# A pruned linear layer on one core: tile 7 of x loaded from GpSimd's queue, and one more late tile stored in halves

## Chip, core and metric

The kernel runs on one core of a Trainium2 chip. A core has a matrix engine (TensorE, "PE" in the profile), a vector engine (VectorE, DVE), a scalar engine (ScalarE, ACT), GpSimd (POOL) and SyncE (SP), and 16 DMA engines that move data between HBM and the on-chip memory (SBUF). Each of SP, ACT and POOL can issue transfers; all of them run on the same 16 DMA engines. The metric is device microseconds for one execution, the median of several runs.

## What is computed

The weights w (1024 x 1024, bf16) are pruned 2:4: of every four consecutive rows, each column keeps the two entries with the largest magnitude. Then x (16 x 512 tokens of 1024 features) is multiplied by the pruned weights and the bias is added.

```python
wg = w.reshape(G, M, D)                 # D = 1024, M = 4, G = 256
mag = jnp.abs(wg)
order = jnp.argsort(mag, 1)
thr = jnp.take_along_axis(mag, order[:, M - N:M - N + 1, :], 1)    # N = 2
mask = (mag >= thr)
wp = (wg * mask).reshape(D, D)
return jnp.einsum("bsd,df->bsf", x, wp) + b
```

## The kernel before

The 8192 tokens are 64 tiles of 128. PE multiplies one tile by the 1024 x 1024 weights in 16 matmuls (eight blocks of 128 features by two halves of 512 output columns), with fp32 sums in PSUM; DVE adds the bias and writes bf16 (`evac`, L400), and ScalarE issues the store of the tile.

Before that can run in a steady loop the weights must be loaded, pruned by DVE and laid out. The prologue works on six pieces of w, numbered 0 to 5: (rows 0 to 511, columns 0 to 255), (the same rows, 256 to 511), and so on. Piece 0 is loaded as four transfers of 64 KB, one for each of the four members m of a group ("u, v, s, t"), two issued by SP and two by ScalarE (L110 to L113). DVE computes magnitudes, maxima, minima, threshold, mask and product of each piece; the product of the first member is the step `mult0u`, written to `wp`.

So that PE has work while later pieces are pruned, the first eight tiles of tokens ("early tiles", 0 to 7) take piece 0 and 1 and so on as they come. Their x is loaded as it lies in HBM, only features 0 to 511 (`load_x`, L103), transposed by PE against an identity matrix into PSUM (`transpose`, L184, the steps "T"), copied to SBUF by ScalarE (`copy_xt`, L192, the steps "C"), and multiplied (`mm_piece`, L205, the steps "M"; M7.0u is tile 7 by the first member of piece 0). Only two PSUM banks serve the transposes, so a third transpose waits for the copy of the first. The x loads of the early tiles are tile 7 (ScalarE), tiles 0 and 1 (ScalarE), tiles 5 and 6 (SP), tile 4 (SP), tiles 2 and 3 (SP). Tiles 5 to 7 are interleaved in groups of three rows in HBM, so that tile 7 is 128 rows of 1 KB.

The order of the work is written out by hand for every engine (`order`, L258) and the program order of each engine is held by `seq` (L64), which also covers the DMA issues of `issue` (L96). PE's list begins

```python
"F8 T7a T5a T6a M7.0u M5.0u M7.0v M5.0v T1a M6.0u M6.0v T0a M7.0s M5.0s M6.0s M7.0t ..."
```

F8 and the calls at L370 and L371 are "fillers": matmuls on constants that give PE something to do from the start. Tile 7 is the first that PE transposes. `make_identity` (L128) makes the identity on GpSimd, with a memset and a select. GpSimd has nothing else to do until it adds the bias to parked sums at L396.

After the prologue, tiles 12 to 63 come in batches, transposed by the DMA on load (`load_nat`, L374). In the last part the loop at L437 stores each tile with one transfer of 256 KB, except that a tile t with t >= NT - LATE is stored in two halves of 512 columns, each as soon as its half is evacuated (L457). The last tile, 63, is cut into four stores. LATE is 5, so tiles 59 to 62 go in halves, and tile 63 in its four parts.

Of the kernel before, what the change touches and what calls it, by code (L numbers as in the profile page):

```python
# [10 lines left out]
def kernel(  # L11
# [7 lines left out]
    nc = tc.nc  # L19
# [20 lines left out]
    NPK = 8  # L40
    LEAD = 4
    GROUPS = ((0, 5), (5, 8))
    LATE = 5
    sizes = (4, 8, 8, 8, 8, 8, 8)
    batches = []
    t0 = NPK + LEAD
# [17 lines left out]
    def seq(eng, inst):  # L64
        if eng in tails:
            tc.add_manual_dep(inst.ins, tails[eng].ins.name, NOSYNC, reason="program order")
        tails[eng] = inst
        return inst
# [22 lines left out]
    def tokens(dram, t):  # L91
        a, b_ = next(s for s in GROUPS if s[0] <= t < s[1])
        return dram[a * P:b_ * P].rearrange("(p t) k -> p t k", p=P), t - a
    bias_sb = const.tile([P, Dout], bf16)

    def issue(eng, out_, in_):  # L96
        q = nc.sync if eng == "sp" else nc.scalar
        return seq(eng, q.dma_start(out_, in_))  # L98

    def load_w(g, c0, c1, ma=0, mb=4, eng="sp"):  # L100
        issue(eng, w_sb[:, g, ma:mb, c0:c1], wv[:, g, ma:mb, c0:c1])

    def load_x(ta, tb, eng="sp"):  # L103
        xs = const.tile([P, tb - ta, HK], bf16, name=f"x_{ta}")
        xv, n = tokens(xf, ta)
        issue(eng, xs[:], xv[:, n:n + tb - ta, :HK])
        for t in range(ta, tb):
            x_sb[t] = xs[:, t - ta, :]

    load_w(0, 0, 256, 0, 1)  # L110
    load_w(0, 0, 256, 1, 2, "act")
    load_w(0, 0, 256, 2, 3)
    load_w(0, 0, 256, 3, 4, "act")  # L113
    load_x(7, 8, "act")
    load_x(0, 2, "act")
    act(nc.scalar.activation(spark[:], nc.const_aps.tensor(1.0, [P, 1], bf16), Act.Abs))
    load_x(5, 7)
# [21 lines left out]
    def spread(g, c0, c1, ks=range(4), eng="sp"):  # L139
        for k in ks:  # L140
            issue(eng, wp_nat[:, 4 * g + k, c0:c1], wp[32 * k:32 * k + 32, g, :, c0:c1])
# [256 lines left out]
    def evac(o, ps, c0, c1, add=None):  # L398
        if add is None:
            dve(nc.vector.tensor_tensor(o[:, c0:c1], ps, bias_sb[:, c0:c1], op=Alu.add))  # L400
        else:
            dve(nc.vector.tensor_tensor(o[:, c0:c1].rearrange("p (n c) -> p n c", n=2),  # L402
                                        ps.rearrange("p (n c) -> p n c", n=2), add, op=Alu.add))
# [7 lines left out]
    def store(eng, t, o, c0=0, c1=Dout):  # L411
        issue(eng, rows(t)[:, c0:c1], o[:, c0:c1])
# [24 lines left out]
    for bi, (tb, nb) in enumerate(batches):  # L437
        if bi:
            load_batch(bi + 1)
        for j in range(nb):  # L440
# [9 lines left out]
            else:  # L450
# [4 lines left out]
                for h in range(2):  # L455
                    evac(o, pss[h][:], h * FH, (h + 1) * FH)
                    if t >= NT - LATE:  # L457
                        store("act", t, o, h * FH, (h + 1) * FH)
                if t < NT - LATE:
                    store("act", t, o)  # L460
# [30 lines left out]
```

## Time and profile before

| | |
|---|---|
| timed runs | 233.79, 233.35, 233.44 us; median 233.44 |
| the profiled execution | 233.83 us, of which the span from first to last instruction is 232.0 us |
| granted TensorE clock | 1.000 (mean) |
| instructions | 2851 |
| HBM read, written | 3.41 MB, 16.78 MB |
| issues of stores `out_dram<-o` | 59 of 256 KB and 8 of 128 KB on ScalarE, 1 of 128 KB on SP, and the small ones of tile 63 |
| x loads | 256 KB by SP twice, 128 KB by SP, 256 KB by ScalarE, 128 KB (tile 7) by ScalarE |

How to read it: the page gives for each engine its busy time and share of the span; for the engines' waits, the time in which an engine was idle and what ended the wait; a chain of waits that is followed back from the last instruction; a timeline of instructions with their start and duration in microseconds from the span's start; and, for stretches of the span, the busy time of each engine and the busy share and rate of the DMA. "L98" is line 98 of the kernel. `SPq` and `ACTq` are the issuing of transfers, `PEld` the weight loads of PE, which overlap its matmuls. The trace also records when each transfer's semaphore increments arrive, that is, when it has landed.

### The profile page before, as it was taken

How to read it: one execution, taken by the hardware profiler on the slowest of the kernel's cores; microseconds unless marked ns; L12 is line 12 of the kernel's file. 1: busy time of each engine (PE TensorE's matmuls, PEld its weight loads, DVE VectorE, ACT ScalarE, POOL GpSimd, SP SyncE). 2: the span in 40 equal slices, each digit the busy share in tenths (PEclk: the TensorE clock that was granted, in tenths of full speed). 3: DMA queues.
4: the chain of work that ended last, by engine and by line, in shares of the span. 5: the costliest groups of instructions: out<-in, count | busy, mean ns of one | idle time of the engine just before them, and what ended most of it. 6: DMA issues, size and time to landing. Idle time of an engine off the chain costs nothing.

```text
span 232.0 us, 2851 instructions
## 1 busy us (share of the span) xinstructions
PE 228.0 (98%) x1158; PEld 112.7 (49%) x1158; DVE 107.9 (46%) x188; ACT 13.4 (6%) x27; POOL 17.6 (8%) x15
## 2 busy tenths in 40 slices
PE   8999999999999999999999999999999999999995
PEld 4887444544444444444444444444444444444443
DVE  4999767754234334334334324424424424423434
ACT  2665100000000000000000000000000000000000
POOL 1000199700000000000000000000000000000000
PEclk9999999999999999999999999999999999999999
DMA  6999999997299321992249821697229942122122
GB/s 192 354 220 211 220 213 227 300 241 272 94 198 275 114 93 51 234 275 76 90 99 250 239 93 47 169 230 198 84 90 191 242 155 76 63 90 81 60 88 90
DMA packets 78268, 38.19 MB, mean 165 GB/s; under 512 B 63664, under 2 KB 70576, under 8 KB 78256
## 3 DMA queue, kind: packets, MB, share of 16 engines
q1 hardware_dynamic: 67328, 20.61, 43.7%
q10 hardware_dynamic: 10928, 17.40, 21.1%
q8 instruction: 9, 0.15, 0.3%
q14 instruction: 3, 0.02, 0.0%
HBM read 3.41 MB, written 16.78 MB: 87 GB/s over the span
## 4 chain that ended last, share of the span: by engine, by line
PE 96%; DMA 2%; ACTq 0%; ACT 0%; DVE 0%; issue 0%
PE ps L239 88%; PE ps L216 6%; DMA x<-in_x_dram 2%; PE tp L239 1%; PE tp L189 1%; ACTq L98 0%; ACT xt L194 0%; DVE o L400 0%
## 5 line engine op out<-in xcount | busy, mean ns | idle before, releaser
L239 PE MATMUL ps<-wp_nat,xb 128*128 128x512 bf16 (+2 forms) x848 | 179.8, 375 | 0.0
L239 PEld LDWEIGHTS <-xb 128*128 128x128 bf16 x848 | 82.4, 98 | 97.5
L400 DVE TENSOR_TENSOR o<-ps,bias_sb 128x512 bf16<-128x512 f32 (+1 forms) x112 | 71.5, 677 | 114.6 <-PE ps L239 114.5
L396 POOL TENSOR_TENSOR st<-st,bias_sb 128x1024 f32<-128x1024 f32 x8 | 16.8, 2131 | 0.0
L216 PE MATMUL ps<-wp,xt 128*128 128x256 bf16 x128 | 15.1, 273 | 0.0
L239 PE MATMUL ps<-wp_nat,xlow 128*128 128x512 bf16 x64 | 14.1, 379 | 0.0
L216 PEld LDWEIGHTS <-xt 128*128 128x128 bf16 x128 | 12.2, 98 | 1.8 <-ACT xt L194 0.2
L402 DVE TENSOR_TENSOR o<-ps,st 128x512 bf16<-128x512 f32 x16 | 11.1, 691 | 2.8 <-PE ps L239 2.3
L239 PE MATMUL ps<-wp_nat,xlead 128*128 128x512 bf16 x48 | 11.2, 379 | 0.0
L239 PEld LDWEIGHTS <-xlow 128*128 128x128 bf16 x64 | 7.2, 112 | 6.7
L239 PEld LDWEIGHTS <-xlead 128*128 128x128 bf16 x64 | 6.3, 98 | 7.1
L256 ACT COPY st<-ps 128x512 f32<-128x512 f32 x16 | 8.5, 598 | 6.3 <-PE ps L216 4.3
L154 DVE TENSOR_TENSOR mag<-mag,hi 128x256 bf16<-128x256 bf16 (+3 forms) x10 | 5.6, 582 | 0.2
L154 DVE TENSOR_TENSOR wp<-w_sb,mag 128x256 bf16<-128x256 bf16 (+3 forms) x10 | 5.6, 580 | 0.1
L133 PE MATMUL ps<-const-bfloat16-1.0 128*128 128x128 bf16 (+1 forms) x22 | 4.3, 394 | 0.8 <-PEq L475 0.8
L164 DVE TENSOR_SCALAR mag<-w_sb 128x512 uint16<-128x512 uint16 (+2 forms) x6 | 2.7, 464 | 3.3 <-DMA w_sb<-in_w_dram 3.3
L239 PE MATMUL tp<-wp_nat,xlead 128*128 128x512 bf16 x16 | 4.1, 379 | 0.0
L133 PEld LDWEIGHTS <-const-bfloat16-1.0 128*128 128x128 bf16 x22 | 2.5, 147 | 2.4 <-issue 2.4
L189 PE MATMUL tp<-ident,x 128*128 128x128 bf16 x32 | 2.9, 219 | 0.6 <-DMA x<-in_x_dram 0.4
L154 DVE TENSOR_TENSOR hi<-mag 128x512 bf16<-128x512 bf16 (+2 forms) x7 | 3.2, 459 | 0.1
L154 DVE TENSOR_TENSOR lo<-mag 128x512 bf16<-128x512 bf16 (+2 forms) x7 | 3.2, 456 | 0.0
L194 ACT COPY xt<-tp 128x256 f32<-128x256 f32 x8 | 2.8, 381 | 3.5 <-PE tp L189 3.5
(15 smaller groups left out, 13.4 us busy)
## 6 DMA issues: line engine op xcount, KB each, us to landing
out_dram<-o ACTq DMA_DIRECT2D x59, 256.0 KB, 2.4
wp_nat<-wp SPq DMA_DIRECT2D x14, 128.0 KB, 3.5
w_sb<-in_w_dram SPq DMA_DIRECT2D x3, 512.0 KB, 6.4
out_dram<-o ACTq DMA_DIRECT2D x8, 128.0 KB, 1.7
x<-in_x_dram SPq DMA_DIRECT2D x2, 256.0 KB, 4.0
w_sb<-in_w_dram SPq DMA_DIRECT2D x1, 256.0 KB, 5.0
x<-in_x_dram ACTq DMA_DIRECT2D x1, 256.0 KB, 4.1
bias_sb<-in_b_dram SPq DMA_DIRECT2D x1, 256.0 KB, 6.4
```

The source lines that it names most:

```text
L133: pe(nc.tensor.matmul(warm_ps[:, :rep * P], lhsT=nc.const_aps.tensor(1.0, [P, P], bf16), rhs=nc.const_aps.tensor(1.0, [P, rep * P], bf16), ...
L154: dve(nc.vector.tensor_tensor(out, a, b_, op=op))
L164: dve(nc.vector.tensor_single_scalar(self.mag[:, ms, :].bitcast(u16), self.w[:, ms, :].bitcast(u16), 0x7FFF, op=Alu.bitwise_and))
L189: pe(nc.tensor.transpose(tp[:, m, :], xg[:, m, :], ident[:]))
L194: act(nc.scalar.copy(xt[:].bitcast(fp32), xpk[t].bitcast(fp32)))
L216: pe(nc.tensor.matmul(ps[:, c0 + d:c1 + d], lhsT=xpk[t][:, m, :], rhs=wp[:, g, m, c0:c1], start=(new and m == ms.start), stop=(left[(q, n) ...
L239: pe(nc.tensor.matmul(ps, lhsT=xt[:, kt - koff, :], rhs=wp_nat[:, kt, c0:c1], start=(kt == first), stop=(kt == last)))
L256: act(nc.scalar.copy(st[:, n % 2, :, :].rearrange("p t c -> p (t c)"), ps_open.pop((q, n))[:]))
L396: pool(nc.gpsimd.tensor_tensor(st[:], st[:], bias[:, :, None, :].to_broadcast([P, 2, 2, CW]), op=Alu.add))
L400: dve(nc.vector.tensor_tensor(o[:, c0:c1], ps, bias_sb[:, c0:c1], op=Alu.add))
L402: dve(nc.vector.tensor_tensor(o[:, c0:c1].rearrange("p (n c) -> p n c", n=2), ps.rearrange("p (n c) -> p n c", n=2), add, op=Alu.add))
```

## The change

Three edits. `issue` learns a third queue, GpSimd's. The load of tile 7 is issued from that queue, and stands first among the loads instead of fifth, where it was the third transfer that ScalarE issued. And LATE goes from 5 to 6, so that tile 58 is stored in halves too.

```diff
-    LATE = 5
+    LATE = 6
...
     def issue(eng, out_, in_):
-        q = nc.sync if eng == "sp" else nc.scalar
+        q = {"sp": nc.sync, "act": nc.scalar, "pool": nc.gpsimd}[eng]
         return seq(eng, q.dma_start(out_, in_))
...
+    load_x(7, 8, "pool")
     load_w(0, 0, 256, 0, 1)
     load_w(0, 0, 256, 1, 2, "act")
     load_w(0, 0, 256, 2, 3)
     load_w(0, 0, 256, 3, 4, "act")
-    load_x(7, 8, "act")
     load_x(0, 2, "act")
     act(nc.scalar.activation(spark[:], nc.const_aps.tensor(1.0, [P, 1], bf16), Act.Abs))
     load_x(5, 7)
```

## The prediction

> **What bounds the kernel now.** First the busy rows of the page: PE is busy 228.0 of 232.0 us, so only time in which PE waits, or its start, can be won.
>
> ```profile
> PE 228.0 (98%) x1158; PEld 112.7 (49%) x1158; DVE 107.9 (46%) x188; ACT 13.4 (6%) x27; POOL 17.6 (8%) x15
> ```
>
> Then the waits of PE. From 11 to 229 us the list is empty; all that there is lies before 11 us:
>
> ```profile
> PE tp L189 <- DMA x<-in_x_dram: 0.4, 1, 0.4
> PE tp L189 <- ACT xt L194: 0.2, 1, 0.2
> ```
>
> So the end is the start of PE's real work plus a fixed stretch of matmuls. The chain of waits, cut to its first 8 us, says what sets that start (start us, us, what):
>
> ```profile
> 0.74 0.41 ACTq L98
> ...
> 1.18 0.46 ACTq L98
> ...
> 1.66 3.79 DMA x<-in_x_dram
> ...
> 5.50 0.43 PE tp L189 x4
> ...
> 5.95 0.38 ACT xt L194
> ...
> 6.38 0.38 PE tp L189 x4
> 6.76 0.44 PE ps L216 x4
> ```
>
> ScalarE issues two pieces of w and then tile 7 of x (at 1.66); that lands at 5.46, PE transposes tile 7 (T7, 5.50), tile 5 (T5), then waits for the copy C7, which frees a PSUM bank, transposes tile 6 (T6, 6.38) and starts the first real matmul, M7.0u, at 6.60. The last filler starts at 4.89 and the next instruction could follow at 4.94. So T7 can move by at most 5.50 - 4.94 = 0.56 us.
>
> Third, the timeline of DVE, because M7.0u also needs the first product mult0u:
>
> ```profile
> 3.27 0.29 DVE L164 TENSOR_SCALAR mag<-w_sb 128x512 uint16<-128x512 uint16 x1 [3.27 <-DMA w_sb<-in_w_dram]
> 3.59 0.29 DVE L154 TENSOR_TENSOR hi<-mag 128x256 bf16<-128x256 bf16 x1
> 3.80 0.29 DVE L164 TENSOR_SCALAR mag<-w_sb 128x512 uint16<-128x512 uint16 x1
> ...
> 5.99 0.48 DVE L154 TENSOR_TENSOR wp<-w_sb,mag 128x256 bf16<-128x256 bf16 x2
> ```
>
> DVE starts when w rows 0 and 1 are in (the second landed at 3.24), and never waits again before 5.99. Its first multiply runs 5.994 to 6.276. That is the second gate, hidden by 0.3 us today.
>
> Fourth, the DMA in stretches of the start (last two columns: busy share of the 16 DMA engines, GB/s):
>
> ```profile
> 2.20:2.90 0.70, 0.70 (x4) 0.19 (x2) 0.00 (x0) 0.26 (x1) 0.00 (x0) 1.00 1.16 315
> 2.90:3.30 0.40, 0.40 (x3) 0.12 (x2) 0.03 (x1) 0.40 (x1) 0.00 (x0) 1.00 0.72 170
> 3.30:3.80 0.50, 0.50 (x6) 0.50 (x5) 0.47 (x2) 0.50 (x1) 0.00 (x0) 1.00 0.89 276
> ```
>
> The engines are full while the w pieces move (2.2 to 2.9), have room from 2.9 to 3.8, and are full again later (358 GB/s from 5.5 to 7.5). An early tile 7 is not free: its 131 KB must pass somewhere.
>
> **The change, step by step.** *Removed:* the issue of tile 7 from ScalarE's queue, 0.454 us. Tiles 0 and 1, issued behind it, go from 2.15 to about 1.66; they landed at 6.26 and were used at 6.93 (slack 0.67): no gain by themselves. The two w issues ahead of it stay.
>
> *Added:* the same 128 rows of 1 KB issued by GpSimd, first thing behind the opening barrier, at about 0.73. No row of before shows a GpSimd transfer. From below: issued by SP at 0.73, a load's first packet moved at 1.82, on ScalarE (0.74) at 2.0; no row has GpSimd quicker than those, so first packets from about 1.9 on. From above: the slowest load of the prologue took 7.2 us to land, so 7.9 at worst in these rows. Nearest is the hardware issue, with some GpSimd work on top (its select over 128x128 took 0.29 us, a 128x1024 add 2.13): I take first packets at 2.4. Eight packets per DMA engine in turn with two other queues (46 + 27 + 27 ns a round) are 0.8 us, and w row 0 landed 0.35 after its last packets: landed at 3.5, give or take 0.5. Anything landed by 4.9 is as good as immediate, for PE is in its fillers until 4.94.
>
> Behind it on GpSimd are only the memset and the select of the identity (0.73 to 1.31 today); T7 needs them at 4.94, so the issue may hold GpSimd 3.6 us at no cost. The bias adds come at 28 us.
>
> *PE after that:* T7 at 4.94, and C7 copied at 5.39 to 5.77 (the copy starts 0.45 after T7 and takes 0.375). T5 needs tiles 5 and 6, landed at 5.15 today: 5.20 (its copy ends 0.85 later and is used at 6.38, so 5.5 would do). T6 at 5.82, and M7.0u would be free at 6.04. Now mult0u ends at 6.276, and with 0.05 us of signal (the copy C7 ended at 6.328, T6 started at 6.379) M7.0u starts at 6.33 instead of 6.60. **The most that the move can win is 0.27 us, not 0.56**; DVE is the bound behind the load. T7 could even start at 5.23 for that.
>
> *Does 0.27 reach the end?* The waits behind M7.0u, their slack from event times in the trace: next multiply 0.34, tile 0 0.67, third multiply 0.62, pieces 1, 2 and 3 of the weights 1.23, 0.97 and 1.18, the spread of piece 3 0.99. Two short waits on C copies (0.18 at 9.86, 0.11 at 10.63) belong to PE's own order and move along. So 0.27 would be kept.
>
> *The price on w.* If tile 7's packets fall between those of w, w lands later by up to 131 KB / 315 GB/s = 0.42 us; by its packets, 8 per DMA engine of 46 ns each, 0.37. Call the delay of DVE's start d; the gain is 0.27 - d. Packets before 2.1 give d = 0.37 to 0.42, a loss of 0.10 to 0.15. At 2.4 us ScalarE's queue had started 78 packets, of 128 for w row 1, so row 1 is late by 0.14; rows 2 and 3 come late by 0.37, but DVE starts on them at 3.80 and they landed by 3.59, so 0.18 of that is covered: d = 0.19. From about 2.8 on, tile 7 falls into the room up to 3.8: d = 0. I take 0.19: gain 0.08.
>
> The Trainium skill speaks against this change: "DMA: Bandwidth & Descriptors", section "Rules for kernel authors", says that spreading transfers over SP, ACT and GpSimd brings no bandwidth and only saves issue time. The 1.16 share at 2.2 to 2.9 agrees with it, the 0.72 right after does not. By the rule alone d would be near 0.4 and the gain gone; by the row alone it is 0.27 for a late enough start.
>
> *SP's queue.* Plain loads take eight semaphores in turn, and the ninth (tile 4) waited for the first: SP stood 0.48 us before 3.26. If tile 7 leaves the turn, tile 4 is the eighth and goes at 2.8; the bias no longer waits for tile 7 (5.46 landed, 5.47 issued). Later loads go up to 0.4 earlier, but behind the same SP loads as now, and their users have the slacks above: 0.
>
> *Tile 58 in halves:* one more issue of 0.338 us on ScalarE, whose queue has 3.45 us per tile there and computes nothing; the first half leaves 0.65 us earlier (one 512-column add). The last landing belongs to tile 63, issued at 229.75. DVE and PE do not wait on stores at the end: 0. The closing list of waits on SP gets one more entry, for GpSimd's transfer; the last such step today took 0.065 us (231.224 to 231.289): 0 to 0.07, and mostly done before the last store lands: 0.
>
> **Sum.** 0.08 us off the profiled execution: span 232.0 to 231.9, its own time 233.83 to 233.75. The three timed runs have a median of 233.44, 0.39 below that execution; the same step from there gives **233.36, say 233.35**.
>
> **Rivals.**
> *A, w is hit in full:* GpSimd is as quick as the hardware queues. For it: the full engines at 2.2 to 2.9. d = 0.37 to 0.42, 233.54 to 233.59. 12%.
> *B, w is not hit:* packets start at 2.8 or later and land by 5.2. For it: the room at 2.9 to 3.8, and that GpSimd's rows are long beside other engines' (that add of 2.13 us). 0.27 off, 233.17. 25%.
> *C, GpSimd is late, the slower side:* the move replaces T7's wait by a longer one for the same tile. It loses from a landing past 5.46 on, one for one, since everything behind it is PE's own order; past 5.93 it is more than 0.47 us (0.2%, about what a measurement of this kernel can tell from no change). With the slowest prologue load's 7.2 us: landed 7.9, +2.5, 235.9. For it: no GpSimd transfer in the trace shows that it is quick. Against: tile 7 has a queue of its own and little to move. 18%.
> The skill's "GPSIMD Engine Reference", section "Instruction dispatch", gives about 6 us for the first call of freshly loaded code; no run here shows it for a transfer, and by it alone (an estimate) tile 7 would land near 9 and the time be about 237.
> *D, the move does not do what it says:* another load lands last. Tiles 5 and 6 share the engines with tiles 0 and 1 earlier; if they come at 5.7 instead of 5.15, T5 goes to 5.75, as today, and all is back at 233.44. Against: less is ahead of them. 5%.
> My forecast has 37%, and 3% are left for a gain over 0.47, for which I see no mechanism.
>
> **Numbers.** B, the forecast, A and D lie within 0.2%: 79%; C nearly all slower. With some room for errors between sessions: faster 0.04, same 0.78, slower 0.18. The range goes from 232.95 (B and 0.2 of scatter; the three runs span 0.44) to 233.95, which takes in the first half microsecond of C.
>
> **What would show it.** After: T7 right behind the fillers near 4.95; no PE wait on x; T6 near 5.8; then PE waits for DVE's wp ahead of M7.0u, which it never did before. DVE's first instruction later than 3.27 by d; M7.0u at 6.33 + d. ScalarE's third issue at 1.66 is tiles 0 and 1; tile 4 at 2.8. PE without waits from 11 us on. Wrong would be: PE waiting for x past 5.46, a wait for the identity, M7.0u ahead of 6.3, or a new wait past 11 us.

## The result, and the profile after

| | before | after |
|---|---|---|
| median of 22 runs each, same chip and session | 233.68 us (233.26 to 234.25) | 234.56 us (233.94 to 236.47) |
| ratio, 95% interval | | 1.0048 [1.0037, 1.0060] |
| the profiled execution, its span | 233.83, 232.0 us | 234.10, 232.3 us |

The change made the kernel slower by about half a percent. The profiled execution of after is one of its quicker ones (0.46 us under the median), so the trace explains the first 0.27 us of the loss and not all of it; more on that below.

First the busy rows and the waits of PE. PE's busy time hardly differs, and there is still no PE wait behind 11 us; the wait for the copy is gone from this list, and the wait for x has doubled from 0.4 to 0.8 us (columns: total, times, longest, in us).

```profile
PE 227.9 (98%) x1158; PEld 112.5 (48%) x1158; DVE 108.0 (47%) x188; ACT 13.4 (6%) x27; POOL 18.3 (8%) x16
```

```profile
PE ps L133 <- PEq L475: 0.8, 1, 0.8
PE tp L189 <- DMA x<-in_x_dram: 0.8, 1, 0.8
```

The chain of waits of after, cut to its first 8 us (start us, us, what):

```profile
0.74 0.39 SPq L98
...
1.19 0.42 SPq L98
...
1.66 4.30 DMA x<-in_x_dram
...
6.00 0.43 PE tp L189 x4
...
6.46 0.38 ACT xt L194
...
6.88 0.50 PE ps L216 x3
```

Before, the chain began on ScalarE's queue (`ACTq`) and its transfer was tile 7. Now it begins on SP's, and the transfer issued at 1.66 is that of tiles 5 and 6. It lands at 5.96, where it landed at 5.15 before. The timeline of PE shows what that does. First before, then after:

```profile
5.50 0.64 PE L189 MATMUL tp<-ident,x 128*128 128x128 bf16 x8 [0.38 <-DMA x<-in_x_dram]
6.38 0.38 PE L189 MATMUL tp<-ident,x 128*128 128x128 bf16 x4 [0.24 <-ACT xt L194]
```

```profile
4.85 0.38 PE L189 MATMUL tp<-ident,x 128*128 128x128 bf16 x4
6.00 0.64 PE L189 MATMUL tp<-ident,x 128*128 128x128 bf16 x8 [0.77 <-DMA x<-in_x_dram]
6.48 0.91 PE L216 MATMUL ps<-wp,xt 128*128 128x256 bf16 x4
```

T7 runs at 4.85, 0.65 earlier than before. Then PE stands until 6.00 for tile 5 (before: T5 at 5.75). M7.0u is even a little earlier (6.48 against 6.60), but M5.0u needs C5, the copy of tile 5, which runs from 6.46 to 6.83. PE's wait for it stands in no list: the views show the matmuls of L216 as one stretch of 0.91 us. By the single matmuls in the trace M5.0u starts at 6.884 instead of 6.708: **0.18 us later**. From there PE's own order carries it to the end: the first matmul of L239 goes from 21.55 to 21.74, the last from 229.17 to 229.36, both 0.19 later. What follows the last matmul took 4.66 us of the profiled execution before and 4.74 after. 0.19 + 0.08 = 0.27, the difference of the two profiled executions.

Two more views. The timeline of GpSimd shows the new transfer and what stands behind it:

```profile
1.23 0.68 POOL L98 DMA_DIRECT2D x<-in_x_dram  x1 [0.78 <-POOLq L475]
1.90 0.22 POOL masks.py:197 MEMSET ident<- 128x128 bf16 x1
2.20 0.29 POOL masks.py:199 TENSOR_SCALAR_AFFINE_SELECT ident<-ident 128x128 bf16<-128x128 bf16 x1
```

And the start of DVE's timeline and its first product, with the DMA in the three stretches that the prediction read (last two columns: busy share of the 16 DMA engines, GB/s):

```profile
3.01 0.29 DVE L164 TENSOR_SCALAR mag<-w_sb 128x512 uint16<-128x512 uint16 x1 [3.01 <-DMA w_sb<-in_w_dram]
...
5.80 0.48 DVE L154 TENSOR_TENSOR wp<-w_sb,mag 128x256 bf16<-128x256 bf16 x2
```

```profile
2.20:2.90 0.70, 0.70 (x4) 0.18 (x2) 0.00 (x0) 0.70 (x1) 0.29 (x1) 1.00 0.99 250
2.90:3.30 0.40, 0.40 (x3) 0.12 (x2) 0.29 (x1) 0.40 (x1) 0.00 (x0) 1.00 1.31 268
3.30:3.80 0.50, 0.50 (x6) 0.50 (x5) 0.47 (x3) 0.35 (x2) 0.00 (x0) 1.00 0.77 215
```

w is not late: DVE starts at 3.01 (3.27 before; 3.06 in e1 below, where the loads stand as before, so this is scatter and no gain of the move). GpSimd's first packet moves only at 2.84, when w has nearly passed. Nor is tile 7 late: landed at 4.57, used at 4.85. The transfer that was moved did what it was meant to do. The one beside it became late.

### The profile page after: what moved, and what is told of

It is laid out like the page before. It is cut to its first block, busy times and chain, and to the rows that moved or that the text cites. A ratio compares the mean times of both kernels' runs of the same rounds, so it can differ in the third digit from the quotient of the medians.

```text
span 232.3 us, 2854 instructions
## 1 busy us (share of the span) xinstructions
PE 227.9 (98%) x1158; PEld 112.5 (48%) x1158; DVE 108.0 (47%) x188; ACT 13.4 (6%) x27; POOL 18.3 (8%) x16
## 3 DMA queue, kind: packets, MB, share of 16 engines
HBM read 3.41 MB, written 16.78 MB: 87 GB/s over the span
## 4 chain that ended last, share of the span: by engine, by line
PE 96%; DMA 2%; SPq 0%; ACT 0%; issue 0%; DVE 0%
PE ps L239 88%; PE ps L216 6%; DMA x<-in_x_dram 2%; PE tp L239 1%; PE tp L189 1%; SPq L98 0%; ACT xt L194 0%; DVE o L400 0%
## 5 line engine op out<-in xcount | busy, mean ns | idle before, releaser
L239 PE MATMUL ps<-wp_nat,xb 128*128 128x512 bf16 (+2 forms) x848 | 179.8, 375 | 0.0
L239 PEld LDWEIGHTS <-xb 128*128 128x128 bf16 x848 | 82.4, 98 | 97.5
L216 PE MATMUL ps<-wp,xt 128*128 128x256 bf16 x128 | 15.2, 273 | 0.1
L239 PE MATMUL ps<-wp_nat,xlow 128*128 128x512 bf16 x64 | 14.1, 379 | 0.0
L216 PEld LDWEIGHTS <-xt 128*128 128x128 bf16 x128 | 12.2, 98 | 2.1 <-ACT xt L194 0.6
L239 PE MATMUL ps<-wp_nat,xlead 128*128 128x512 bf16 x48 | 11.2, 379 | 0.0
L239 PEld LDWEIGHTS <-xlow 128*128 128x128 bf16 x64 | 7.2, 112 | 6.7
L239 PEld LDWEIGHTS <-xlead 128*128 128x128 bf16 x64 | 6.2, 98 | 7.1
L239 PE MATMUL tp<-wp_nat,xlead 128*128 128x512 bf16 x16 | 4.1, 379 | 0.0
```

The source lines that it names most:

```text
L216: pe(nc.tensor.matmul(ps[:, c0 + d:c1 + d], lhsT=xpk[t][:, m, :], rhs=wp[:, g, m, c0:c1], start=(new and m == ms.start), stop=(left[(q, n) ...
L239: pe(nc.tensor.matmul(ps, lhsT=xt[:, kt - koff, :], rhs=wp_nat[:, kt, c0:c1], start=(kt == first), stop=(kt == last)))
```

## The experiments

The question was what holds tiles 5 and 6 back. Three theories were put against each other. **Neighbours:** tile 7 left a place on ScalarE's queue, tiles 0 and 1 moved up into it (issued at 1.67 instead of 2.15), so tiles 5 and 6 now share the DMA engines with two other queues at a time instead of one. **GpSimd's transfer itself:** its 4 KB packets hold the engines, whatever else moves. **Chance:** the landing is that of the slowest of 16 DMA engines and scatters. Beside these stood a fourth part, for the slowest runs: PE's longer idle stretch meets the clock's grant. The theory of neighbours stands here as it was in the end. At first it spoke only of tiles 0 and 1 moving up; that a transfer of GpSimd counts as a neighbour like any other came in behind e8 (the expectation of e9 is the first that says it).

Each experiment is given as a ratio to the kernel before, run on the same chip in the same session.

### e1, the stores alone

```diff
-    LATE = 5
+    LATE = 6
```

> Before, with six late tiles in halves and nothing else. All theories: the store of tile 58 hides behind 3.4 us of matmuls, so within 0.1% of the kernel before (233.5 to 233.9 where that has 233.7), PE without waits from 11 us on, M7.0u at 6.60.

Measured: 233.88 us against 233.75, ratio 1.0007 [0.9998, 1.0016]. Six late tiles cost nothing that shows. The trace also gives a second look at the old order of loads: tiles 5 and 6 landed at 5.10, and tile 7 at 5.23 where the first trace had 5.46, so M7.0u came at 6.37 instead of 6.60, and the first matmul of L239 at 21.32 instead of 21.55. Two lessons: a landing scatters by 0.2 us and more, and PE's start is carried one for one.

### e2, the load alone

```diff
-    LATE = 6
+    LATE = 5
```

(against the changed kernel.)

> The change without the sixth late tile. Theory 'packets' (tile 7's 4 KB packets from GpSimd hold the DMA engines around 3 us, so that tiles 5 and 6 land at 5.96 instead of 5.15 and T5 is late) and rival 'order' (tiles 0 and 1 now move beside tiles 5 and 6): the whole effect is here, ratio 1.003 to 1.006, tiles 5 and 6 landing at 5.8 or later. If the sixth late tile were the cause: within 0.1% of before.

Measured: 234.67, ratio 1.0039 [1.0027, 1.0052]. The whole loss is in the moved load. Waits and chain of PE in this run:

```profile
PE tp L189 <- DMA x<-in_x_dram: 1.3, 1, 1.3
```

```profile
1.65 4.58 DMA x<-in_x_dram
...
6.27 0.43 PE tp L189 x4
```

Tiles 5 and 6 landed at 6.22; M5.0u started at 7.15, 0.44 later than before.

### e3, another tile on GpSimd

The kernel before, with tile 7 left on ScalarE and tile 4 issued by GpSimd first.

```diff
+    load_x(4, 5, "pool")
     load_w(0, 0, 256, 0, 1)
...
     load_w(0, 256, 512)
-    load_x(4, 5)
     load_x(2, 4)
```

> Tile 7 back on ScalarE as in before; GpSimd loads tile 4 first instead, the same 128 rows of 1 KB, which nobody needs until 8.9 us. 'Packets': tiles 5 and 6 and tile 7 start some 0.5 us late all the same and land near 5.7 to 6.0, T7 near 5.9, ratio 1.001 to 1.004. 'Order': tiles 5 and 6 stand beside tile 7 as in before and land at 5.15 to 5.3, T7 at 5.5, ratio within 0.1%. Rival 'fixed' (any GpSimd transfer costs at the end of the program or spreads the times): slower by 0.3% or more with loads landing as in before.

Measured: 235.90, ratio 1.0092 [1.0079, 1.0106], the slowest of all. Here all early loads are late: tile 7 at 5.86, tiles 5 and 6 at 6.17. But that is 0.4 for tile 7, and the loss is 2.15 us. The rest is the clock of PE, which shows in the pace of matmuls. The timeline of this run, then that of the kernel before for the same steps:

```profile
5.91 1.66 PE L189 MATMUL tp<-ident,x 128*128 128x128 bf16 x12 [0.70 <-DMA x<-in_x_dram]
7.36 1.06 PE L216 MATMUL ps<-wp,xt 128*128 128x256 bf16 x4
```

```profile
6.60 0.60 PE L216 MATMUL ps<-wp,xt 128*128 128x256 bf16 x4
```

Four matmuls take 1.06 us instead of 0.60; singly they start 0.213 us apart instead of 0.109, and the transposes 0.107 instead of 0.056. The quick pace comes only at 9.37; in the trace of before it came at 4.90, in that of after at 4.66. These are the instants at which the trace's own records of the granted clock begin. The views print 1.00 for the time ahead of them too, so their rows don't show the slow stretch; the pace of like instructions does. On tiles 5 and 6 the run went against the theory of order as it then stood (5.15 to 5.3 expected) and with that of GpSimd's transfer (5.7 to 6.0). It does not tell whether that transfer does more than any other neighbour, and its time is that of the clock, so it asked for e5 and for e7.

### e5, the same with PE kept busy

```diff
-            "F8 T7a T5a T6a M7.0u M5.0u M7.0v M5.0v T1a M6.0u M6.0v T0a M7.0s M5.0s M6.0s M7.0t M5.0t M6.0t "
+            "F16 T7a T5a T6a M7.0u M5.0u M7.0v M5.0v T1a M6.0u M6.0v T0a M7.0s M5.0s M6.0s M7.0t M5.0t M6.0t "
```

(against e3: 16 fillers ahead of T7 instead of 8.)

> The kernel with tile 4 on GpSimd (235.9) with eight more fillers ahead of T7. There the fillers ended at 4.94, T7 came at 5.91, and PE's clock was granted only at 9.37 us instead of 4.9. 'Clock' (PE idle for a good part of the stretch before the grant delays it by 3.4 us): the fillers now reach 5.8, the clock is granted by about 6.5, and the time falls by 1.2 to 2 us to 233.9 to 234.7. Rival 'loads' (the late loads alone cost the 2 us): 235.6 to 236.1 as before.

Measured: 234.39, ratio 1.0029 [1.0020, 1.0038]. The loads were as late as in e3 (tile 7 at 5.89, tiles 5 and 6 at 6.21), yet about 1.5 us came back. The timeline:

```profile
5.21 0.84 PE L133 MATMUL ps<-const-bfloat16-1.0 128*128 128x128 bf16 x6
5.94 0.87 PE L189 MATMUL tp<-ident,x 128*128 128x128 bf16 x8
7.01 0.38 PE L189 MATMUL tp<-ident,x 128*128 128x128 bf16 x4 [0.20 <-ACT xt L194]
7.24 0.60 PE L216 MATMUL ps<-wp,xt 128*128 128x256 bf16 x4
```

The transposes begin at the slow pace and take the quick one from about 6.5; the first real matmuls are back at 0.60 for four. So idle time of PE in the first six microseconds can cost far more than its own length. It need not: in e4 and e12 below PE stood 0.57 and 0.54 us behind T7, and the quick pace came by 6.4 all the same. The line of e12:

```profile
6.17 0.69 PE L189 MATMUL tp<-ident,x 128*128 128x128 bf16 x8 [0.54 <-DMA x<-in_x_dram]
```

How long the idle time must be, and when, no run here shows. The Trainium skill's "TensorE: Matmul & The Clock Gate", section "Part 1: The HAM clock gate", says that full speed is granted after a busy window of about 3.4 us, and that the windows run free of the kernel. That fits: in e3 PE stood 0.7 us behind the fillers and the pace changed at 9.37. By an estimate with the page's window (3413 ns), 9.37 less 3.41 is 5.96, just after PE took up work again at 5.91. The traces also agree with windows that run free: the quick pace came at 4.90 in before and at 3.72 in e1, though the program is the same for PE's fillers up to there.

### e6, after with PE kept busy

```diff
-            "F8 T7a T5a T6a M7.0u M5.0u M7.0v M5.0v T1a M6.0u M6.0v T0a M7.0s M5.0s M6.0s M7.0t M5.0t M6.0t "
+            "F8 T7a F9 T5a T6a M7.0u M5.0u M7.0v M5.0v T1a M6.0u M6.0v T0a M7.0s M5.0s M6.0s M7.0t M5.0t M6.0t "
```

(against the changed kernel.)

> The changed kernel with nine fillers between T7 and T5, where PE stood idle 0.8 us or more for tiles 5 and 6. 'Clock': the runs at 235.2 to 236.5 (6 of 22 before) are gone, median 234.2 to 234.5. 'Loads': the spread stays, some runs at or over 235.2, median 234.6.

Measured: 234.23, ratio 1.0025 [1.0016, 1.0034], and no run of the 12 above 234.64, where the changed kernel had 6 of 22 at 234.9 or more (and e10 below two at 236.1 and 236.8). Tiles 5 and 6 still landed at 6.20 and M5.0u came at 7.12. The fillers did not take the loss away, for they move no load; what they seem to take is its slow tail. See under what stays open.

### e4, tile 7 not loaded at all

The kernel before without the load of tile 7: zeros stand in its place, so one early tile's part of the input is left out.

```diff
+    x7c = const.tile([P, HK], bf16, name="x7c")
+    pool(nc.gpsimd.memset(x7c[:], 0.0))
+    x_sb[7] = x7c[:]
...
-    load_x(7, 8, "act")
     load_x(0, 2, "act")
```

> The change without any load of tile 7: PE transposes a constant tile of zeros in its place, so tile 7's output is the bias plus other features only. Tiles 0 and 1 are third on ScalarE as in the change, and no GpSimd transfer exists. 'Packets': tiles 5 and 6 land by 5.2, T5 right behind T7, M7.0u near 6.3 where DVE lets it go: 0.27 us faster than before, ratio 0.9985 to 0.9995. 'Order': tiles 5 and 6 land at 5.7 or later although GpSimd moves nothing, and the time is not below before's.

Measured: 234.07, ratio 1.0011 [1.0002, 1.0020]. With 128 KB less to move and no transfer on GpSimd, it is no faster. In its trace, of one of the slower of its runs (234.35 of 233.56 to 234.38), 15 of the 16 semaphore increments of tiles 5 and 6 were in by 5.34, the last came at 6.15, and T5 with it. This was a blow to the theory on GpSimd's packets, which are absent here, and in favour of chance for this one trace.

### e7, tiles 0 and 1 taken out of the way

The changed kernel, with tiles 0 and 1 issued by SP behind tiles 5 and 6, so that beside these only GpSimd's tile 7 moves.

```diff
-    load_x(0, 2, "act")
     act(nc.scalar.activation(spark[:], nc.const_aps.tensor(1.0, [P, 1], bf16), Act.Abs))
     load_x(5, 7)
+    load_x(0, 2)
```

> The changed kernel with tiles 0 and 1 issued by SP behind tiles 5 and 6, so that they don't move beside them. 'Neighbour' (tiles 0 and 1, at once third on ScalarE, take the engines' turns from tiles 5 and 6): tiles 5 and 6 land by 5.3, T5 by 5.4, M7.0u near 6.3, ratio 0.998 to 1.000. 'Packets' (GpSimd's 4 KB packets do it): tiles 5 and 6 land at 5.6 or later all the same, ratio 1.002 or more.

Measured: 233.70 against 233.64, ratio 1.0003 [0.9993, 1.0012]. The loss is gone, with GpSimd's transfer still there. All PE waits of this run, and the timeline:

```profile
PE ps L133 <- PEq L475: 0.8, 1, 0.8
```

```profile
5.00 1.48 PE L189 MATMUL tp<-ident,x 128*128 128x128 bf16 x12
6.32 0.82 PE L216 MATMUL ps<-wp,xt 128*128 128x256 bf16 x4
```

The list has no wait for x, but the single transposes have a short one, under 0.2 us: T7's last starts at 5.32 and T5's first at 5.60, right behind the landing of tiles 5 and 6 at 5.55. (5.3 was expected with neighbours, 5.6 or later with GpSimd's packets: the landing lies between, and the time decides.) The transposes run at the slow pace in the beginning (1.48 us for twelve). M7.0u comes at 6.32, close to the 6.33 that the prediction had for an undisturbed w, though it is the slow pace that sets it here; M5.0u comes at 6.64. **This is the pair that decides: the same GpSimd transfer, 1.0048 (1.0030 in a later session, e10) with tiles 0 and 1 abreast of tiles 5 and 6, and 1.0003 with tiles 0 and 1 behind them.** In the same session as e7, e6 with the order of loads of the change measured 1.0025 [1.0016, 1.0034].

### e8 and e9, the same move without GpSimd

e8 is e4 (tile 7 left out) and e9 is the kernel before (tile 7 on ScalarE), both with tiles 0 and 1 behind tiles 5 and 6 on SP, the diff of e7.

> As the kernel without a load of tile 7 (zeros stand in its place), with tiles 0 and 1 issued by SP behind tiles 5 and 6: tiles 5 and 6 have the DMA for themselves after w. 'Neighbour': they land by 5.0, M7.0u at 6.3, 0.27 us faster than before, ratio 0.9985 to 0.9995. If they land at 5.8 or later here too, then neither neighbour nor GpSimd is needed for it, and a single slow DMA engine or the issue itself is the cause.

> The kernel before with tiles 0 and 1 issued by SP behind tiles 5 and 6, tile 7 third on ScalarE as it was; no GpSimd transfer. Tiles 5, 6 and 7 then have the engines for themselves after w. 'Neighbours' (each other stream beside tiles 5 and 6 adds some 0.5 us to their landing): half of their increments by 4.8, all landed by 5.3, tile 7 by 5.2; T7 right behind the fillers, M7.0u at 6.3 to 6.4, ratio 0.998 to 0.9995, the fastest version here. If tile 7 still lands at 5.4 or later: ratio 1.000, and what limits it is not the neighbours but the slowest DMA engine.

Measured: e8 233.75, ratio 1.0008 [0.9997, 1.0019]; e9 233.86, ratio 1.0015 [0.9995, 1.0035]. In e8, with nothing beside them, tiles 5 and 6 landed at 4.50, and PE met the second gate of the prediction. Three of its waits (line numbers are two higher, for the kernel has two lines more):

```profile
PE tp L191 <- DMA x<-in_x_dram: 0.7, 1, 0.7
PE tp L191 <- ACT xt L196: 0.2, 1, 0.2
PE ps L218 <- DVE wp L156: 0.2, 1, 0.2
```

The last row is the wait for `mult0u`: M7.0u starts at 6.08, right behind it. But the first row is a new wait for tiles 2 and 3, which landed at 9.71, a single late increment (the fifteenth came at 8.68), and it gives the gain back. e9 had the same on a smaller scale, tiles 2 and 3 at 9.51 and 0.2 us of wait. Both were expected to gain, e9 as the fastest version of all; neither did. In e9 tiles 5 and 6 landed at 5.49 (5.3 expected), and M7.0u came at 6.39.

### e11 and e12, tiles 2 and 3 taken off the end of SP's list

To cure that, the order of e9 (e11) and of e7 (e12) with tiles 2 and 3 issued by ScalarE. The diff is e11's against the kernel before; e12 makes the same moves in the changed kernel.

```diff
-    load_x(0, 2, "act")
     act(nc.scalar.activation(spark[:], nc.const_aps.tensor(1.0, [P, 1], bf16), Act.Abs))
+    load_x(2, 4, "act")
     load_x(5, 7)
+    load_x(0, 2)
     load_w(0, 256, 512)
     load_x(4, 5)
-    load_x(2, 4)
```

> The kernel before with two moves of loads and nothing on GpSimd: tiles 0 and 1 issued by SP behind tiles 5 and 6, tiles 2 and 3 issued by ScalarE behind its table load. Theory of neighbours (the landing of tiles 5 and 6 grows by about 0.5 us for each queue that moves beside them): beside them are tile 7 and then tiles 2 and 3, so about what there was before, tiles 5 and 6 at 5.0 to 5.6, tile 7 at 5.1 to 5.5, tiles 2 and 3 by 8.5 instead of 9.5, so no wait of PE for x after 6; M7.0u at 6.3 to 6.6 and a ratio of 0.998 to 1.000 to the kernel before. Rival (what counts is the slowest of the 16 DMA engines, which lags by chance, whatever the order of the issues): tiles 5 and 6 at 5.9 or later or one of the later tiles waited for, ratio 1.000 to 1.003.

> The changed kernel with the same two moves: tile 7 by GpSimd first, tiles 0 and 1 by SP behind tiles 5 and 6, tiles 2 and 3 by ScalarE behind its table load. Theory of neighbours: ScalarE's queue now issues tiles 2 and 3 right behind w, at about 1.7 to 3, so tiles 5 and 6 again have two neighbours as in the change (GpSimd's tile 7, ScalarE's 2 and 3) if that issue goes before 3, and land at 5.9 to 6.2, ratio 1.002 to 1.005; if ScalarE's table load holds the issue back past 3.5, one neighbour at a time, tiles 5 and 6 at 5.4 to 5.7, M7.0u at 6.3 to 6.4, ratio 0.998 to 1.000. Rival (a transfer on GpSimd's queue is what harms, whatever stands beside it): 1.002 to 1.005 in both cases, and slower than the same order without GpSimd by 0.003 or more.

Measured: e11 235.27, ratio 1.0041 [1.0006, 1.0077]; e12 234.02, ratio 1.0007 [0.9982, 1.0031]; before 233.69, with 4 of its 23 runs at about 236, hence the wide intervals and ratios lower than those of the medians (1.0067 and 1.0014). In e11 tile 7 and tiles 5 and 6 came as expected (5.49 and 5.47), but tiles 2 and 3 landed at 9.21 and piece 1 of w at 9.43 (15 of 16 increments by 7.71). DVE stood 2.4 us for that piece (its timeline), and PE had two waits for x:

```profile
9.45 0.43 DVE L164 TENSOR_SCALAR mag<-w_sb 128x1024 uint16<-128x1024 uint16 x1 [2.40 <-DMA w_sb<-in_w_dram]
```

```profile
PE tp L189 <- DMA x<-in_x_dram: 1.6, 2, 1.0
```

My expectation for e11 was a gain, and it failed on late last increments, for which the rival had allowed (if not for so much: 1.000 to 1.003). In e12 ScalarE's issue went at 1.73, so tiles 5 and 6 again had two queues beside them; they landed at 6.13, within the 5.9 to 6.2 expected for that branch. The time was better than expected for it (1.0007, but with an interval to 1.0031; its median is 0.33 us above before's). That e12 is not slower than e11 says little against GpSimd's transfer, since e11 was held up by late loads of its own. Neither version beats the kernel before.

### e10, the change again

The changed kernel, unaltered, in another session.

> The changed kernel once more, unchanged, for another trace and more runs beside the one above. 'Neighbours' and 'clock' together: tiles 5 and 6 land at 5.9 to 6.4, tile 7 by 4.6; median 234.4 to 234.8, some runs over 235. If it is one accident of one profile: tiles 5 and 6 land by 5.4 here.

Measured: 234.14 against 233.80, ratio 1.0030 [1.0005, 1.0055]. The landing of tiles 5 and 6 repeats, at 6.02, and so does the wait, longer now because T7 came at 4.47:

```profile
PE tp L189 <- DMA x<-in_x_dram: 1.2, 1, 1.2
```

M5.0u at 6.95 is 0.24 later than before; the profiled execution (234.16) is near the median of these runs.

## What the traces say of tiles 5 and 6 together

Each transfer's semaphore gets 16 increments, as many as there are DMA engines, and they are read here as one of each. The middle of the 16 (mean of the eighth and ninth) tells of the typical engine, the last is the landing. Over all fourteen traces, by how many other queues moved x beside tiles 5 and 6 (issued at 1.64 to 1.66 in every one):

| beside tiles 5 and 6 | kernels | middle increment, us | landing, us |
|---|---|---|---|
| nothing | e8 | 4.31 | 4.50 |
| one queue at a time | before, e1, e4, e7, e9, e11 | 4.86, 4.86, 4.78, 4.80, 4.83, 4.97 | 5.15, 5.10, 6.15, 5.55, 5.49, 5.47 |
| two queues | after, e2, e10, e6, e12, e3, e5 | 5.34, 5.12, 5.21, 5.06, 5.35, 5.24, 5.82 | 5.96, 6.22, 6.02, 6.20, 6.13, 6.17, 6.21 |

The three groups of the middle column don't overlap, and it makes no difference whether the one queue beside is GpSimd's (e7) or ScalarE's (before, e1, e9): the means of the groups are 4.31, 4.85 and 5.30, so a further queue costs the typical engine about half a microsecond. Four orders make a square: neither neighbour 4.31 (e8), GpSimd's tile 7 alone 4.80 (e7), ScalarE's tiles 0 and 1 alone 4.78 (e4), both 5.06 to 5.34 (after, e2, e6, e10). GpSimd's 128 KB cost as much as ScalarE's 256 KB, so these two traces show no effect of a neighbour's bytes. The grouping was made after most of these runs; of those made to test it, e10 and e12 (5.9 to 6.4 and 5.9 to 6.2 expected) and e11 (5.0 to 5.6) landed as it said, e9 0.2 late. Every landing with two queues lies between 5.96 and 6.22, every one with one queue, e4 excepted, between 5.10 and 5.55. On top of the middle comes the lag of the slowest engine, 0.2 to 1.4 us. The neighbours thus set the middle, and the lag scatters without a cause that was found: both theories had a part. GpSimd's transfer weighs as one neighbour, no more and no less. In all seven kernels with two queues beside, one of the two is GpSimd's; a pair without it was not run.

The Trainium skill's "DMA: Bandwidth & Descriptors", section "Issuing engines are not separate DMA queues", states that transfers of all issuing engines run on the same 16 DMA engines and interleave. The table agrees, and adds what the third queue costs the others.

## Why the prediction was wrong

It said 233.35 us, the same as before; it came out slower, past its range.

- **The step that failed** is "T5 needs tiles 5 and 6, landed at 5.15 today: 5.20". It kept the landing of a transfer that had not been touched. But the change took tile 7 from between w and tiles 0 and 1 on ScalarE's queue, and these went from 2.15 to 1.67, abreast of tiles 5 and 6. The prediction noted the move and called it "no gain by themselves"; its sum did not ask whom it costs. Measured: 5.96 to 6.22 in the four traces with this order of loads (after, e2, e6, e10), 0.8 to 1.1 late.
- **Rival D** named this mechanism and got 5%. The argument against it, "less is ahead of them", counted what lies ahead on the queues and not what moves beside. Its limit was also too mild: with 5.7 it came back to 233.44, while the real landing went beyond.
- **The slack of T5** was right: "its copy ends 0.85 later". 5.96 and 0.05 of signal and 0.85 make 6.86 for the end of C5; it ended at 6.83, and M5.0u started at 6.88. From this sentence the loss could have been computed.
- **T7 right behind the fillers near 4.94**: right, at 4.85.
- **GpSimd's first packets at 2.4, landing 3.5, give or take 0.5**: mis-sized. The issue began at 1.23, took 0.68, the first packet moved at 2.84 and tile 7 landed at 4.57. It cost nothing, since PE was in its fillers. C, on which the chance of a slower kernel (0.18) stood almost alone, did not come: that the kernel was slower is no credit to it.
- **w late by 0.19**: wrong in size, 0. Its four transfers landed at 2.81, 2.99, 3.38 and 3.58 (3.00, 3.24, 3.41 and 3.59 before); e1, without the move, had 2.83, 3.04, 3.34 and 3.53.
- **DVE is the bound behind the load, and 0.27 the most to win**: not reached in after, where `mult0u` was done before PE came. In e8 it is the wait that PE meets, at 6.08 (`mult0u` was itself earlier there than the 6.276 of the first trace), and in e7 M7.0u came at 6.32 by another cause, the slow pace. So the gate is real; the gain of 0.27 was never seen in a time.
- **The start is kept to the end**: right. The shifts of the first matmul of L239 and of the last one agree within 0.01 in all traces but e8 and e11, which lose another 0.12 and 0.21 us between the two.
- **SP's tile 4 at 2.8, no wait of PE from 11 us on, halves of tile 58 for nothing**: right (2.84; none; e1). The closing wait list grew by one entry; what follows the last matmul took 4.66 to 4.81 us over the traces, 4.79 and 4.81 with five late tiles (e2, e3) and 4.77 without GpSimd (e1), so no cost can be assigned to it.

**What stays open.** The chain accounts for 0.27 us in the profiled execution of after, and for 0.33 in that of e10 (234.16 against the same 233.83), near e10's 0.34 of medians. The first session lost 0.88. Its runs have a tail at 235 to 236.5, one of them at a mean granted clock of 0.993; e10 has one too (236.1 and 236.8, both at 0.993, and one run of 237.9 that its ratio leaves out), and e6, with PE kept busy, has none. That PE's idle stretch between T7 and T5 (0.8 to 1.3 us) meets the clock's window in some runs is therefore likely, but argued: no execution of the tail was traced, idle time of 0.5 to 0.6 us in e4 and e12 brought no such delay, and the kernel before had such runs too in one session (4 of 23), though none in the 101 runs of the other four. Why the last increment comes 0.7 to 1.7 us behind the fifteenth in some transfers (tiles 2 and 3 in e8 and e9, tiles 5 and 6 in e4, piece 1 of w in e11) was not found either.

## What to carry to other kernels

When a transfer leaves a queue, look at what moves up into its place, and at whom that lands beside: the loss here came to the one load that the diff does not touch. Judge an early load by everything that is in flight with it, and keep the load that is needed next with at most one neighbour, by issuing less urgent ones behind it on its own queue (e7: from 1.0048 to 1.0003). And a start that is brought forward is worth nothing when the next operand is not there. It may be worth less than nothing, for PE then idles where its clock is being granted; e3 against e5 shows that such idle time can cost 1.5 us, and for the change itself it is argued.

## What the runs showed that I had not expected

- A GpSimd load of 128 KB: issue 0.5 us later than those of SP and ScalarE (1.23 against 0.74), 0.68 us of GpSimd instead of about 0.45, first packet 1.6 us after the issue began, landing 3.0 to 4.0 us after it (e12 and e5 the ends); its 32 packets are of 4 KB. The queue row of after shows 48 packets in all; by the trace's packet records the other 16 are of 4 bytes (packets, MB, share).

```profile
q0 software_dynamic: 48, 0.13, 0.3%
```

- 0.7 us of PE idle at the wrong moment of the start delayed the quick pace from about 4.9 to 9.37 and cost 1.5 us (e3 against e5), with nothing in the profile's row of granted clock. Without any change to PE's program up to there, that instant also moved from 4.90 (before) to 3.72 (e1).
- Of the landing of a 256 KB load, 0.2 to 1.4 us lie between the middle and the last of its 16 increments.
